# Holding two loads behind crossbar transposes, and another order for pairs 2 to 4, in a fused linear-attention and MLP kernel

## The chip, the cores and the metric

The kernel runs on one core of a Trainium2 chip. The metric is the device time of one execution in microseconds, as the median of several runs. Beside it there is the profile of one execution.

The engines are called TensorE (PE in the profile; its weight loads PEld), VectorE (DVE), ScalarE (ACT), GpSimd (POOL) and SyncE (SP). Each takes its instructions in order. A wait at the head of an engine's queue holds everything behind it.

## The reference

Two computations follow each other. The first is a gated linear attention over 4 batches, 8 heads, 768 tokens and head size 48:

```python
for t in range(S):
    state = alpha[:, :, t, :, None] * state + np.einsum('bhd,bhe->bhde', k[:, :, t], v[:, :, t])
    y[:, :, t] = np.einsum('bhd,bhde->bhe', q[:, :, t], state)
```

Its result, with the heads side by side, is x with 3072 rows of 384 numbers. The second is an MLP over these rows: `gelu(x @ w_in) @ w_out`, with an inner width of 2048 and the tanh form of GELU. Inputs and output are 32-bit floats in the chip's DRAM.

## The kernel before

**Tiles.** The 768 tokens are cut into 6 chunks of 128. A chunk of two batches is a pair: pair m is chunk m // 2 with batches 0 and 1 (m even) or 2 and 3 (m odd). There are 12 pairs, 0 to 11.

**Work of a pair.** The tiles a, q, k and v are loaded. `ln` takes the logarithm of a (tile la), `cum` sums it over the tokens with a matmul, and `b` and `binv` are the exponentials of the sum and of its negative. From these come q' = q * b (`qp`) and k' = k * binv (`kp`). q' and k' are transposed, on TensorE with a copy to SBUF for pairs 0 to 5 (`t`, `ev`, the tile qkT), and by a DMA transpose through the crossbar for pairs 6 to 11 (`turn6.0` is q' of pair 6, `turn6.1` its k', `turn6.2` its x). `attn` multiplies k' with q' (tile at) and q' with the state carried from the chunk before (tile yps), `mask` puts zeros above the diagonal (atm), `y` adds atm times v to yps, and `x` copies the result to SBUF, in two halves. `kv`, `tr` and `st` make the next state. x is transposed, on TensorE (`tx`, `xe`) or by the crossbar, into the tile xT.

**The MLP.** It runs per chunk in blocks of one batch (chunk 0) or two. `l1` is the first matrix product, in groups of six matmuls of 128x256 into the tile hT; `gelu` writes gT; `l2` is the second product in groups of four matmuls of 128x384 into the tile acc; `ot` copies acc to an output tile, and `store` writes that to DRAM. In a name like `l210.3` the digits after `l2` are the chunk, the first batch and the group; `ot03.0` is the output tile of chunk 0, batch 3.

**Buffers.** There are four PSUM buffers ff (for hT, acc and half of at), one ca of two banks (for cum and the other half of at), two yk; five SBUF buffers each for a, q, k, v and ot, and three xT.

**Order.** Nothing is scheduled by a tool. The list `FIRST` names each step with its engine (P, V, A, G, S for PE, DVE, ACT, POOL, SP), and each engine takes its steps in the order of the list. Semaphores between the engines follow from which tile each step reads and writes. ScalarE changes between a table with the logarithm and the exponential and one with GELU, at the steps where the list asks for it.

**Loads.** GpSimd issues all loads from pair 2 on, and a good part of the stores. It has eight semaphores for its transfers, used in turn, so that a transfer waits for the landing of the eighth before it. `LOADS` sets which tiles are loaded in which rows, and what they wait for: after `window 3` each load has a `gate` ahead of it, a copy of one element out of the tile that was loaded three loads earlier. GpSimd so waits until that tile has landed, and no more than three loads are under way.

Of the kernel before, what the change touches and what calls it, by code (L numbers as in the profile page):

```python
# [76 lines left out]
class _Kernel:  # L77
# [5 lines left out]
             "aqkv 3", "aqkv 4", "aqkv 5", "window 3", "aqkv 6", "aqkv 7", "aqkv 8", "aqkv 9", "aqkv 10", "aqkv 11")  # L83
# [24 lines left out]
        V:mask3.0 V:mask3.2 A:ln4.0 P:l211.1 P:l210.0 P:l211.2 P:y3.1 P:cum4.0 P:y3.0 P:l210.1 P:l211.3 V:x3.0 A:x3.1 A:b4.0 A:ln5.0 A:binv4.0
        A:ot11.0 P:tx3.0 P:tx3.1 P:l210.2 V:qp4.0 V:xe3.0 V:xe3.1 V:tr4.0 P:kv3.1 P:cum5.0 P:l210.3 P:l112.0 P:l112.1 V:st3.1 V:kp4.0 P:t4.0 V:tr4.2
        V:tr4.1 V:ev4.0 V:tr4.3 V:ev4.1 A:b5.0 A:ot10.0 A:binv5.0 P:l112.4 P:l112.7 A:gelu12.0 A:gelu12.1 P:kv4.0 P:l112.5 P:kv4.1 P:l112.3 A:gelu12.7  # L110
        A:gelu12.4 A:gelu12.3 A:gelu12.5 V:st4.0 V:st4.1 P:l112.6 A:gelu12.6 P:l112.2 P:attn4.0 G:gate.a6.0 G:load.v6.0 G:gate.q6.0 G:load.a7.0
        G:gate.k6.0 G:load.q7.0 G:store11.0 G:gate.v6.0 G:load.k7.0 G:gate.a7.0 G:load.v7.0 G:gate.q7.0 G:load.a8.0 G:gate.k7.0 V:kp5.0 V:tr5.0
        A:gelu12.2 P:l212.0 P:l212.1 V:mask4.2 V:mask4.0 V:mask4.1 P:l212.2 P:y4.0 P:l212.3 V:mask4.3 P:y4.1 A:ln6.0 P:cum6.0 A:x4.0 P:l213.0 V:tr5.1
        V:qp5.0 A:ot12.0 A:x4.1 P:tx4.0 V:xe4.0 A:binv6.0 P:tx4.1 V:xe4.1 P:l213.1 P:t5.0 V:kp6.0 V:ev5.0 A:b6.0 P:l213.2 P:l213.3 V:tr6.0 A:ev5.1
        P:attn5.0 V:tr6.1 G:store02.0 A:ln7.0 V:ot13.0 V:mask5.0 V:mask5.1 P:l120.0 V:mask5.2 V:tr6.2 V:mask5.3 P:l120.2 V:tr5.2 V:tr5.3 A:gelu20.0
        A:gelu20.2 P:l120.6 P:l120.7 A:gelu20.6 P:l120.1 A:gelu20.1 P:y5.0 V:x5.0 P:l120.4 A:gelu20.7 A:gelu20.4 P:l120.5 P:l120.3 A:gelu20.5 V:qp6.0
        V:tr6.3 G:load.q8.0 G:gate.v7.0 G:load.k8.0 S:turn6.1 A:gelu20.3 P:cum7.0 P:y5.1 V:x5.1 P:l221.0 P:kv5.0 P:l220.0 P:tx5.1 P:l221.1 V:st5.0
        G:gate.a8.0 G:load.v8.0 G:gate.q8.0 G:load.a9.0 V:xe5.1 A:b7.0 P:l220.1 P:tx5.0 P:kv6.0 V:qp7.0 V:xe5.0 S:turn6.0 P:l221.2 V:st6.0 P:kv5.1
        A:binv7.0 S:turn7.0 V:st5.1 A:ln8.0 P:cum8.0 A:binv8.0 A:b8.0 P:l221.3 P:l220.2 P:l220.3 A:ot21.0 P:attn6.0 V:kp7.0 A:ot20.0 P:l122.0 P:l122.2
        G:store21.0 V:mask6.0 V:mask6.1 V:mask6.2 V:mask6.3 P:l122.7 A:gelu22.0 A:gelu22.2 P:l122.4 V:tr7.0 V:tr7.1 G:store13.0 G:store12.0 P:y6.0  # L120
        A:gelu22.4 A:gelu22.7 P:l122.1 P:y6.1 A:gelu22.1 A:x6.0 P:l122.6 V:x6.1 P:l122.3 G:store10.0 P:kv6.1 V:st6.1 P:l122.5 P:l223.0 A:gelu22.3
        P:l223.1 A:gelu22.6 A:gelu22.5 P:l223.2 S:turn7.1 G:store20.0 S:turn6.2 G:gate.k8.0 V:qp8.0 G:load.q9.0 P:l222.0 V:tr7.2 V:tr7.3 V:kp8.0
        P:l222.1 S:turn8.0 P:attn7.0 V:mask7.2 V:mask7.3 P:l223.3 A:ln9.0 P:l222.2 P:l222.3 G:gate.v8.0 G:load.k9.0 G:gate.a9.0 G:load.v9.0
        G:gate.q9.0 G:load.a10.0 G:gate.k9.0 G:load.q10.0 G:gate.v9.0 V:mask7.0 V:mask7.1 A:ot23.0 A:ot22.0 P:cum9.0 P:l130.0 P:y7.0 P:l130.2 P:y7.1
        P:l130.4 V:x7.0 A:binv9.0 V:x7.1 V:tr8.0 V:tr8.1 A:gelu30.0 A:gelu30.2 P:l130.1 A:gelu30.4 A:gelu30.1 P:l130.3 V:kp9.0 A:gelu30.3 P:l130.5
        P:kv7.0 A:gelu30.5 P:l130.7 S:turn8.1 A:gelu30.7 G:load.k10.0 G:gate.a10.0 G:load.v10.0 G:gate.q10.0 G:load.a11.0 P:l130.6 P:kv7.1 P:l231.0
        V:st7.1 P:l231.1 P:l230.0 P:l230.1 A:gelu30.6 A:b9.0 V:tr8.2 V:tr8.3 V:st7.0 P:l231.2 P:l231.3 A:ot31.0 P:l230.2 P:l230.3 A:ot30.0 V:tr9.0
        V:qp9.0 G:gate.k10.0 S:turn7.2 P:attn8.0 P:l132.0 P:l132.5 V:mask8.0 V:mask8.1 P:l132.7 P:l132.2 V:mask8.2 V:mask8.3 V:tr9.1 A:gelu32.0 P:y8.0
        A:gelu32.5 A:gelu32.7 S:turn9.1 S:turn9.0 G:store30.1 P:l132.1 P:y8.1 P:l132.3 P:l132.6 V:x8.0 A:gelu32.2 P:l132.4 P:kv9.0 A:x8.1 V:tr9.2
        V:tr9.3 V:st9.0 A:gelu32.1 A:gelu32.3 A:gelu32.4 P:l232.0 P:l232.1 A:gelu32.6 P:l232.2 P:kv8.1 P:kv8.0 P:l233.0 P:l233.1 S:turn8.2 G:store23.0  # L130
        A:ln10.0 P:cum10.0 A:b10.0 G:store31.1 S:store30.0 V:st8.1 V:st8.0 S:store22.0 S:store31.0 A:binv10.0 V:qp10.0 P:l232.3 A:ot32.0 P:l233.2
        P:l233.3 V:ot33.0 P:attn9.0 A:ln11.0 P:l140.0 V:mask9.0 V:mask9.1 V:mask9.2 P:l140.7 P:l140.4 A:gelu40.0 A:gelu40.4 A:gelu40.7 V:kp10.0
        V:mask9.3 P:l140.1 P:l140.2 P:y9.0 P:l140.3 S:store32.1 S:turn10.0 A:gelu40.1 A:gelu40.3 S:turn10.1 V:x9.0 A:gelu40.2 P:y9.1 P:l240.0 A:x9.1
        P:l140.5 A:gelu40.5 P:l240.1 P:l140.6 P:kv9.1 V:st9.1 A:gelu40.6 P:l240.2 P:cum11.0 P:l240.3 S:turn9.2 G:load.q11.0 G:gate.v10.0 G:load.k11.0
        G:gate.a11.0 V:ot40.0 A:b11.0 P:l241.0 P:l241.1 P:l241.2 P:l241.3 G:store40.0 A:binv11.0 V:qp11.0 V:ot41.0 P:l142.0 P:attn10.0 V:mask10.0
        V:mask10.1 P:l142.5 A:gelu42.0 A:gelu42.5 P:l142.3 P:l142.6 A:gelu42.3 P:l142.2 A:gelu42.2 A:gelu42.6 P:l142.1 V:kp11.0 A:gelu42.1 S:turn11.0
        S:store41.0 S:turn11.1 P:l142.7 V:mask10.2 P:y10.0 V:mask10.3 P:y10.1 P:l142.4 P:l242.0 A:x10.0 A:x10.1 S:turn10.2 P:l243.0 P:l242.1
        A:gelu42.4 A:gelu42.7 P:l243.1 P:l242.2 P:l242.3 P:l243.2 P:l243.3 G:load.v11.0 A:ot42.0 S:store33.1 S:store32.0 P:attn11.0 V:ot43.0
        V:mask11.0 V:mask11.1 P:l150.0 P:l150.1 P:l150.6 A:gelu50.0 A:gelu50.1 A:gelu50.6 P:l150.4 P:l150.3 A:gelu50.3 V:mask11.2 V:mask11.3 P:y11.0
# [110 lines left out]
    def wait(self, r, m, j):  # L250

        u = self.p[list(self.p)[m]]
        return lambda e: self.nc.gpsimd.tensor_copy(self.gate[:, 0:1], u["T"][:, j, 0, 0, 0:1] if r == "T" else u["vb" if r == "v" else r][:, j, 0, 0:1])
# [385 lines left out]
    def tasks(self):  # L639
# [8 lines left out]
        loads, held = self.loads()  # L648
# [222 lines left out]
```

## Time and profile before

| | us |
|---|---|
| median of 3 runs | 173.23 |
| lowest, highest | 173.20, 173.99 |
| the profiled execution | 173.67 |
| its span, first to last instruction | 171.9 |
| TensorE busy in the span | 166.4 |
| VectorE busy | 108.7 |
| ScalarE busy | 126.4 |
| GpSimd busy | 74.0 |

How to read the profile: an entry of a timeline gives the start from the span's begin, the length, the engine, the line of the kernel, and what is written from what. Neighbours of the same kind are merged (x12), and the idle time of the engine ahead of an entry stands in square brackets with what ended it. Matmuls are pipelined, so that the length of one entry overlaps the start of the next by some 0.17 us. What TensorE loses shows in the distance from one start to the next. For a DMA, the entry is its issue, and its landing is told by the view of a tile. POOLq and SPq are the parts of an engine that only issue and wait.

### The profile page before, as it was taken

What the parts mean: (1) busy time and instruction counts of PE and PEld (TensorE: products, weight loads), DVE (VectorE), ACT (ScalarE), POOL (GpSimd) and SP (SyncE); (2) the same over time, 40 slices, a digit from 0 to 9 for tenths busy, and PEclk for the clock granted to TensorE, in tenths of its full rate; (3) what the DMA queues carried; (4) which work ended last, traced back from release to release, by engine and by line L of the source; (5) the groups of instructions that cost most, each with busy time, mean ns of one, the idle gap of its engine ahead of it and who ended that gap; (6) DMA issues with size and microseconds to landing.
All of it is one profiled execution on the core that took longest, in us unless ns stands there. A gap on an engine that the chain in (4) does not pass through costs nothing.

```text
span 171.9 us, 4766 instructions
## 1 busy us (share of the span) xinstructions
PE 166.4 (97%) x1998; PEld 131.5 (76%) x1998; DVE 108.7 (63%) x207; ACT 126.4 (74%) x203; POOL 74.0 (43%) x105
## 2 busy tenths in 40 slices
PE   7999999999999999999999899999999999999992
PEld 2678998567976886797696597796796895987971
DVE  6599602699997999999978666766944730620000
ACT  4696879896797989889788398587978682454740
POOL 6598458976238786841193614227000400100000
PEclk9999999999999999999999999999999999999998
DMA  4999999999999899999499999999962793130103
GB/s 134 286 231 174 228 251 259 233 212 194 262 235 185 209 176 233 205 205 149 92 264 222 129 148 217 78 141 285 254 105 50 91 191 95 46 91 5 46 24 115
DMA packets 54213, 29.01 MB, mean 169 GB/s; under 512 B 43728, under 2 KB 50176, under 8 KB 54192
## 3 DMA queue, kind: packets, MB, share of 16 engines
q0 software_dynamic: 31296, 19.96, 73.4%
q1 hardware_dynamic: 22352, 8.36, 25.4%
q10 hardware_dynamic: 544, 0.39, 0.8%
q8 instruction: 15, 0.25, 0.6%
q14 instruction: 6, 0.05, 0.1%
HBM read 25.17 MB, written 4.72 MB: 174 GB/s over the span
## 4 chain that ended last, share of the span: by engine, by line
PE 81%; DVE 7%; DMA 5%; ACT 4%; issue 1%; DVEq 0%; ACTq 0%
PE hT L557 34%; PE acc L576 28%; DMA xT<-x 5%; PE at L446 3%; PE idle L228 3%; PE cum L285 2%; PE yps L525 2%; PE kv L475 2%; PE xT_ps L515 1%; DVE atm L465 1%; PE cum L317 1%; DVE tr L489 1%; PE qkT_ps L364 1%; DVE kp L354 1%; DVE stmp L500 1%
## 5 line engine op out<-in xcount | busy, mean ns | idle before, releaser
L557 PE MATMUL hT<-xT,w_in 128*128 128x256 bf16 (+1 forms) x672 | 69.8, 258 | 0.5 <-DMA xT<-x 0.5
L576 PE MATMUL acc<-w_out,gT 128*128 128x384 bf16 (+3 forms) x416 | 68.2, 314 | 0.0
L563 ACT ACTIVATE gT<-hT 128x512 bf16<-128x512 f32 x96 | 52.9, 599 | 16.1 <-PE hT L557 14.9
L557 PEld LDWEIGHTS <-w_in 128*128 128x128 bf16 x672 | 61.8, 113 | 1.9 <-DMA xT<-x 0.9
L576 PEld LDWEIGHTS <-gT 128*128 128x128 bf16 x416 | 37.4, 98 | 20.5
L465 DVE TENSOR_TENSOR atm<-at,ut 128x512 bf16<-128x512 f32 x48 | 30.3, 684 | 2.8 <-PE at L446 2.7
L601 POOL DMA_DIRECT2D out_dram<-ot x15 | 8.4, 562 | 32.9 <-DVE ot L588 25.6
L588 DVE COPY ot<-acc 128x384 f32<-128x384 f32 (+1 forms) x10 | 5.2, 523 | 25.9 <-PE acc L576 25.6
L588 ACT COPY ot<-acc 128x384 f32<-128x384 f32 (+2 forms) x16 | 7.3, 458 | 13.0 <-PE acc L576 9.5
L500 DVE TENSOR_TENSOR stmp<-kv,st 128x384 f32<-128x384 f32 x16 | 8.9, 557 | 9.1 <-PE kv L475 8.6
L489 DVE STREAM_TRANSPOSE tr<-b 32x256 f32<-32x256 f32 x32 | 14.0, 438 | 0.8
L247 POOL DMA_DIRECT2D a<-in_alpha_dram x11 | 12.2, 1112 | 4.6 <-issue 1.7
L354 DVE TENSOR_TENSOR kp<-k,binv 128x768 bf16<-128x768 f32 (+1 forms) x15 | 11.9, 794 | 2.6 <-DMA k<-in_k_dram 1.9
L247 POOL DMA_DIRECT2D k<-in_k_dram x11 | 12.3, 1118 | 2.9 <-issue 1.3
L219 ACT ACT_TABLE_LOAD x10 | 12.8, 1283 | 0.9 <-PEq L855 0.7
L247 POOL DMA_DIRECT2D vb<-in_v_dram x11 | 12.2, 1107 | 2.5 <-DMA q<-in_q_dram 1.0
L247 POOL DMA_DIRECT2D q<-in_q_dram x11 | 12.3, 1115 | 1.7 <-DMA w_in<-in_moe_w_in_dram 1.0
L563 ACT ACT_TABLE_LOAD x10 | 12.8, 1283 | 0.2
L354 DVE TENSOR_TENSOR qp<-q,b 128x768 bf16<-128x768 f32 (+1 forms) x15 | 11.9, 795 | 0.9 <-ACT b L343 0.6
L343 ACT ACTIVATE b<-cum 128x768 f32<-128x768 f32 (+1 forms) x15 | 10.1, 684 | 2.6 <-PE cum L317 2.2
L343 ACT ACTIVATE binv<-cum 128x768 bf16<-128x768 f32 (+1 forms) x15 | 10.3, 688 | 2.2 <-PE cum L317 1.3
L535 DVE CAST x<-yps 128x384 bf16<-128x384 f32 x12 | 6.5, 555 | 6.1 <-PE yps L525 6.0
(75 smaller groups left out, 156.8 us busy)
## 6 DMA issues: line engine op xcount, KB each, us to landing
a<-in_alpha_dram POOLq DMA_DIRECT2D x9, 384.0 KB, 9.4
q<-in_q_dram POOLq DMA_DIRECT2D x9, 384.0 KB, 7.3
k<-in_k_dram POOLq DMA_DIRECT2D x9, 384.0 KB, 8.0
out_dram<-ot POOLq DMA_DIRECT2D x12, 192.0 KB, 4.0
vb<-in_v_dram POOLq DMA_DIRECT2D x9, 192.0 KB, 6.8
w_in<-in_moe_w_in_dram POOLq DMA_DIRECT2D x4, 384.0 KB, 8.6
w_out<-in_moe_w_out_dram POOLq DMA_DIRECT2D x4, 384.0 KB, 9.9
out_dram<-ot SPq DMA_DIRECT2D x7, 192.0 KB, 2.1
```

What stands on the lines that cost most here:

```text
L219: nc.scalar.add_instruction(mybir.InstLoadActFuncSet(name=nc.get_next_instruction_name(), act_func_set_id=i, engine=mybir.EngineType.Activ ...
L247: dma(u[t][:, lo:hi].rearrange("t b h d -> t (b h) d"), src.rearrange("b h s d -> s (b h) d")[c * C:(c + 1) * C])
L343: self.nc.scalar.activation(u[n].rearrange("t i h d -> t i (h d)")[:, lo:hi], cum, AF.Exp, scale=1.0 if n == "b" else -1.0)
L354: self.nc.vector.tensor_tensor(out, rows, b, op=ALU.mult)
L465: self.nc.vector.tensor_tensor(u["atm", i][:, o], u["at", i][o], self.ut[:, None, :].to_broadcast([self.C, self.H // 2, self.C]), op=ALU.mult)
L489: self.nc.vector.transpose(u["tr"][f:f + 32, :, 0:32], rows[:, lo:lo + H * 2 * D].rearrange("t (g n) -> t g n", n=2 * D)[:, :, 0:32])
L500: nc.vector.tensor_tensor(s, acc, old, op=ALU.add)
L557: self.nc.tensor.matmul(h[:, s].rearrange("p (g t) -> p g t", t=self.C), w_in[:, j, nt % 4 + s], self.xT[c % self.NX][:, lo:hi, j], start= ...
L563: return lambda e: self.nc.scalar.activation(self.gT[c % self.NG][:, nt:nt + 4 // (hi - lo), lo * self.C:hi * self.C], f.pop(("h", c, lo, ...
L576: self.nc.tensor.matmul(f["acc", c, b][:, lo:hi], self.gT[c % self.NG][:, nt, b * self.C:(b + 1) * self.C], self.w_out[:, nt, lo:hi], star ...
L588: self.copy(e)(f["ot", c, b][:, sl], f["acc", c, b] if half is None else f["acc", c, b, half][:, sl])
L601: return lambda e: (self.nc.sync if e == "SP" else self.nc.gpsimd).dma_start(self.out[r:r + self.C, sl], f["ot", c, b][:, sl])
```

## The change

Three things change. First, the steps of the list between the transposes of pair 2 and the MLP's second block of chunk 1 stand in another order: on TensorE, VectorE and ScalarE groups change places, and five copies that VectorE made are made by ScalarE (the output tiles `ot01`, `ot02`, `ot03`, the second half of x of pair 2, the first half of x of pair 3). The stores of the output tiles 00, 03 and 11 are issued by SyncE and not by GpSimd. Second, GpSimd loads a, q, k and v pair by pair from pair 3 on, and `window 3` begins with pair 8 and not with pair 6, so that the tiles of pairs 6 and 7 are loaded without a gate. Third, two new gates stand in GpSimd's queue: `gate.T6.0` reads the transposed q' of pair 6 ahead of the load of a of pair 9, and `gate.X6.0` reads the transposed x of pair 6 ahead of the loads of k and v of pair 9. All later steps stay as they are.

```diff
@@ LOADS
-             "aqkv 3", "aqkv 4", "aqkv 5", "window 3", "aqkv 6", "aqkv 7", "aqkv 8", "aqkv 9", "aqkv 10", "aqkv 11")
+             "aqkv 3", "aqkv 4", "aqkv 5", "aqkv 6", "aqkv 7", "window 3", "aqkv 8", "gate T 6 0", "aq 9", "gate X 6 0", "kv 9", "aqkv 10", "aqkv 11")
@@ FIRST
...
-        G:store03.0 G:gate.v5.0 G:load.k6.0 S:store01.0 V:qp3.0 P:tx2.0 P:tx2.1 P:l202.3 V:xe2.0 V:xe2.1 P:kv2.0 P:l110.0 P:l110.7 P:l110.1 V:kp3.0
...
+        V:xe2.1 V:xe2.0 P:kv2.0 P:l110.0 P:l110.6 V:kp3.0 V:st2.0 V:tr3.0 V:tr3.1 P:l110.5 A:ot02.0 A:gelu10.0 A:gelu10.6 P:t3.0 S:store00.0 P:l110.3
...
@@ def wait(self, r, m, j):
-        return lambda e: self.nc.gpsimd.tensor_copy(self.gate[:, 0:1], u["T"][:, j, 0, 0, 0:1] if r == "T" else u["vb" if r == "v" else r][:, j, 0, 0:1])
+        c, i = list(self.p)[m]
+        src = {"T": lambda: u["T"][:, j, 0, 0, 0:1], "X": lambda: self.xT[c % self.NX][:, 2 * i, 0, 0:1]}.get(r, lambda: u["vb" if r == "v" else r][:, j, 0, 0:1])
+        return lambda e: self.nc.gpsimd.tensor_copy(self.gate[:, 0:1], src())
@@ def tasks(self):
                 xts[c, 2 * i] = xts[c, 2 * i + 1] = xe
+                if ("X", m, 0) in held:
+                    held["X", m, 0].deps.append(xe)
```

On VectorE, from the state rows of pair 2 (`tr`) to the first state of pair 2 (`st`), the order before was this; b_100 belongs to pair 3, kp_98 is its k', and xT_104 is the xT tile of chunk 1:

```order
L489 STREAM_TRANSPOSE tr<-b_99 32x8x32 x4
L588 COPY ot<-acc 128x384 x2
L465 TENSOR_TENSOR atm<-at,ut 128x512 x4
L588 COPY ot<-acc 128x384
L535 CAST x<-yps 128x8x48 x2
L354 TENSOR_TENSOR qp_94<-q,b_100 128x16x48
L548 COPY xT_104<-xT_ps 128x384 x2
L354 TENSOR_TENSOR kp_98<-k,binv 128x16x48
L500 TENSOR_TENSOR stmp<-kv,st_1_81 128x384
L502 TENSOR_TENSOR st_0_80<-stmp,tr 128x384
L588 COPY ot<-acc 128x384
```

And this is the same stretch in the changed kernel (its lines are numbered one higher):

```order
L490 STREAM_TRANSPOSE tr<-b_99 32x8x32 x4
L589 COPY ot<-acc 128x384
L466 TENSOR_TENSOR atm<-at,ut 128x512 x4
L536 CAST x<-yps 128x8x48
L355 TENSOR_TENSOR qp_94<-q,b_100 128x16x48
L549 COPY xT_104<-xT_ps 128x384 x2
L355 TENSOR_TENSOR kp_98<-k,binv 128x16x48
L501 TENSOR_TENSOR stmp<-kv,st_1_81 128x384
L503 TENSOR_TENSOR st_0_80<-stmp,tr 128x384
```

Three copies of output tiles and one half of x have left this stretch. On ScalarE the stretch from the transposes of pair 2 to the first GELU of chunk 1 was this before (la_88, b_100 and binv are of pair 3, gT_107 is of chunk 1):

```order
L385 COPY qkT<-qkT_ps 128x16x64 x2
L219 ACT_TABLE_LOAD
L300 ACTIVATE la_88<-a 128x16x48
L343 ACTIVATE b_100<-cum 128x768
L343 ACTIVATE binv<-cum 128x768
L563 ACT_TABLE_LOAD
```

In the changed kernel it reads:

```order
L386 COPY qkT<-qkT_ps 128x16x64 x2
L589 COPY ot<-acc 128x384
L218 ACT_TABLE_LOAD
L301 ACTIVATE la_88<-a 128x16x48
L344 ACTIVATE b_100<-cum 128x768
L536 CAST x<-yps 128x8x48
L344 ACTIVATE binv<-cum 128x768
L589 COPY ot<-acc 128x384 x2
L564 ACT_TABLE_LOAD
```

The four copies stand here, one ahead of the logarithm and three ahead of the first GELU. On GpSimd, from the load of v of pair 8 to that of v of pair 9, the order before was this; ot x5 are five stores:

```order
L247 DMA vb<-in_v_dram 128x16x48
L253 COPY gate<-q 128x1
L247 DMA a<-in_alpha_dram 128x16x48
L601 DMA out_dram<-ot 128x384 x5
L253 COPY gate<-k 128x1
L247 DMA q<-in_q_dram 128x16x48
L253 CAST gate<-vb 128x1
L247 DMA k<-in_k_dram 128x16x48
L253 COPY gate<-a 128x1
L247 DMA vb<-in_v_dram 128x16x48
```

And in the changed kernel:

```order
L246 DMA vb<-in_v_dram 128x16x48
L254 CAST gate<-qkT 128x1
L254 COPY gate<-q 128x1
L246 DMA a<-in_alpha_dram 128x16x48
L602 DMA out_dram<-ot 128x384 x5
L254 COPY gate<-k 128x1
L246 DMA q<-in_q_dram 128x16x48
L254 CAST gate<-xT_103 128x1
L254 CAST gate<-vb 128x1
L246 DMA k<-in_k_dram 128x16x48
L254 COPY gate<-a 128x1
L246 DMA vb<-in_v_dram 128x16x48
```

The two gates on qkT and xT_103 are new; everything behind them in GpSimd's queue, the five stores and the loads of pair 10 too, waits until they pass.

More of the change, by code (lines that the diff above doesn't have):

```diff
@@ L108 @@
[L108 to L139, printed above, removed]
@@ new lines @@
+        P:tx3.0 V:xe3.0 V:tr4.1 P:cum5.0 G:load.a7.0 G:load.q7.0 G:load.k7.0 G:load.v7.0 G:gate.q7.0 G:load.a8.0 G:gate.k7.0 A:b5.0 S:store03.0
+        P:l210.3 P:l112.0 P:l112.7 S:store11.0 A:ot10.0 A:binv5.0 V:kp4.0 A:gelu12.0 A:gelu12.7 V:tr4.2 V:tr4.3 P:t4.0 V:ev4.0 P:l112.3 P:l112.5
+        V:ev4.1 P:kv4.0 P:l112.4 A:gelu12.3 P:kv4.1 A:gelu12.5 A:gelu12.4 V:st4.0 P:l112.6 A:gelu12.6 S:store01.0 P:l112.1 P:l112.2 A:gelu12.1 V:st4.1
+        V:tr5.0 V:kp5.0 P:attn4.0 A:gelu12.2 P:l212.0 P:l212.1 V:mask4.2 V:mask4.0 V:mask4.1 P:l212.2 P:y4.0 P:l212.3 V:mask4.3 P:y4.1 A:ln6.0
@@ new lines @@
+        P:cum6.0 A:x4.0 P:l213.0 V:tr5.1 V:qp5.0 A:ot12.0 A:x4.1 P:tx4.0 V:xe4.0 A:binv6.0 P:tx4.1 V:xe4.1 P:l213.1 P:t5.0 V:kp6.0 V:ev5.0 A:b6.0
+        P:l213.2 P:l213.3 V:tr6.0 A:ev5.1 P:attn5.0 V:tr6.1 G:store02.0 A:ln7.0 V:ot13.0 V:mask5.0 V:mask5.1 P:l120.0 V:mask5.2 V:tr6.2 V:mask5.3
+        P:l120.2 V:tr5.2 V:tr5.3 A:gelu20.0 A:gelu20.2 P:l120.6 P:l120.7 A:gelu20.6 P:l120.1 A:gelu20.1 P:y5.0 V:x5.0 P:l120.4 A:gelu20.7 A:gelu20.4
+        P:l120.5 P:l120.3 A:gelu20.5 V:qp6.0 V:tr6.3 G:load.q8.0 G:gate.v7.0 G:load.k8.0 S:turn6.1 A:gelu20.3 P:cum7.0 P:y5.1 V:x5.1 P:l221.0 P:kv5.0
@@ new lines @@
+        P:l220.0 P:tx5.1 P:l221.1 V:st5.0 G:gate.a8.0 G:load.v8.0 V:xe5.1 A:b7.0 P:l220.1 P:tx5.0 P:kv6.0 V:qp7.0 V:xe5.0 S:turn6.0 G:gate.T6.0
+        G:gate.q8.0 G:load.a9.0 P:l221.2 V:st6.0 P:kv5.1 A:binv7.0 S:turn7.0 V:st5.1 A:ln8.0 P:cum8.0 A:binv8.0 A:b8.0 P:l221.3 P:l220.2 P:l220.3
+        A:ot21.0 P:attn6.0 V:kp7.0 A:ot20.0 P:l122.0 P:l122.2 G:store21.0 V:mask6.0 V:mask6.1 V:mask6.2 V:mask6.3 P:l122.7 A:gelu22.0 A:gelu22.2
+        P:l122.4 V:tr7.0 V:tr7.1 G:store13.0 G:store12.0 P:y6.0 A:gelu22.4 A:gelu22.7 P:l122.1 P:y6.1 A:gelu22.1 A:x6.0 P:l122.6 V:x6.1 P:l122.3
@@ new lines @@
+        G:store10.0 P:kv6.1 V:st6.1 P:l122.5 P:l223.0 A:gelu22.3 P:l223.1 A:gelu22.6 A:gelu22.5 P:l223.2 S:turn7.1 G:store20.0 S:turn6.2 G:gate.k8.0
+        V:qp8.0 G:load.q9.0 G:gate.X6.0 P:l222.0 V:tr7.2 V:tr7.3 V:kp8.0 P:l222.1 S:turn8.0 P:attn7.0 V:mask7.2 V:mask7.3 P:l223.3 A:ln9.0 P:l222.2
+        P:l222.3 G:gate.v8.0 G:load.k9.0 G:gate.a9.0 G:load.v9.0 G:gate.q9.0 G:load.a10.0 G:gate.k9.0 G:load.q10.0 G:gate.v9.0 V:mask7.0 V:mask7.1
+        A:ot23.0 A:ot22.0 P:cum9.0 P:l130.0 P:y7.0 P:l130.2 P:y7.1 P:l130.4 V:x7.0 A:binv9.0 V:x7.1 V:tr8.0 V:tr8.1 A:gelu30.0 A:gelu30.2 P:l130.1
@@ L145 @@
+        P:l152.0 P:l152.5 A:gelu52.0 A:gelu52.5 P:l152.2 A:gelu52.2 P:l152.1 A:gelu52.1 P:l152.3 A:gelu52.3 P:l152.7 P:l152.4 P:l152.6 A:gelu52.4
+        P:l252.0 P:l252.1 P:l252.2 A:gelu52.7 A:gelu52.6 P:l252.3 S:store50.0 A:ot52.0 S:store52.0 S:store51.0 P:l253.0 P:l253.1 A:ot53.0 S:store53.0
+        P:l253.2 P:l253.3 P:l253.4 A:ot53.1 S:store53.1 P:l253.5 V:ot53.2 G:store43.0 S:store53.2
     """.split()
```

34 lines of the change are left out of this document (23 added, 11 removed).

## The prediction

> **What bounds the kernel now.** I read the page first, for the engine that is full.
>
> ```profile
> core 0: 171.9 us, clock 0.996
> ```
> ```profile
> PE 166.4 (97%) x1998; PEld 131.5 (76%) x1998; DVE 108.7 (63%) x207; ACT 126.4 (74%) x203; POOL 74.0 (43%) x105
> ```
>
> TensorE is busy for 166.4 of 171.9 us at a clock of 0.996, and the change removes none of its instructions. So it can gain only the moments in which TensorE stands still or stretches, and it can lose by adding such moments. The list of TensorE's waits has one inside the program that is not its start:
>
> ```profile
> PE hT L557 <- DMA xT<-x: 0.5, 1, 0.5
> ```
>
> The chain of waits from 84 to 120 us says where this is. Its third column is the length of a piece; I also take the unit prices of eight yps matmuls (0.20) and of six hT matmuls (0.67) from it.
>
> ```profile
> 88.28 0.20 PE yps L525 x8
> 88.48 0.67 PE hT L557 x6
> ...
> 90.29 8.05 DMA xT<-x
> ```
>
> From 90.29 on the chain is one transfer: the crossbar transpose of pair 6's x, 8.05 us from its issue to its landing. TensorE's own timeline shows what it cost:
>
> ```profile
> 97.39 0.49 PE L317 MATMUL cum<-la,ut_h 128*128 128x384 f16 x2
> 98.38 0.85 PE L557 MATMUL hT<-xT,w_in 128*128 128x256 bf16 x6 [0.51 <-DMA xT<-x]
> ```
>
> The second place is no wait by name. In the chain from 48 to 70 us the path leaves TensorE and runs through VectorE, piece after piece, from the first row below to the second, before it comes back:
>
> ```profile
> 54.19 0.96 DVE qp L354
> ...
> 64.81 2.50 DVE atm L465 x4
> ...
> 67.62 0.33 PE cum L317 x2
> 67.95 0.65 PE acc L576 x4
> ```
>
> The stretch from 36 to 68 us, in which pairs 2 to 4 are worked on, has this row (length, then busy time of PE, PEld, DVE, ACT, POOL, each with its count, then clock, DMA share and GB/s):
>
> ```profile
> 36.00:68.00 32.00, 31.79 (x427) 24.43 (x425) 29.71 (x54) 26.95 (x39) 20.75 (x27) 1.00 1.28 215
> ```
>
> VectorE is busy for 29.71 of 32 us, ScalarE for 26.95. VectorE has hardly a gap left, and TensorE's rows show small stretches where it hands over late:
>
> ```profile
> 60.22 0.82 PE L557 MATMUL hT<-xT,w_in 128*128 128x256 bf16 x6
> 61.09 0.33 PE L475 MATMUL kv<-vb,kp 128*128 128x96 bf16 x4
> ...
> 64.07 2.12 PE L576 MATMUL acc<-w_out,gT 128*128 128x384 bf16 x12
> 66.15 0.37 PE L525 MATMUL yps<-vb,atm 128*128 128x48 bf16 x8
> 66.36 0.81 PE L576 MATMUL acc<-w_out,gT 128*128 128x384 bf16 x4
> 67.01 0.61 PE L525 MATMUL yps<-vb,atm 128*128 128x48 bf16 x8
> 67.46 0.48 PE L317 MATMUL cum<-la,ut_h 128*128 128x384 f16 x2
> ```
>
> **The change, part by part.** *The gate on x of pair 6.* Two cum matmuls take 0.33 us, so the first hT group of chunk 3 could have begun at 97.39 + 0.33 = 97.72; it began at 98.38. That is 0.66 us lost. While the crossbar is under way, GpSimd's timeline has these loads:
>
> ```profile
> 89.24 1.17 POOL L247 DMA_DIRECT2D k<-in_k_dram  x1
> 90.41 0.20 POOL L253 COPY gate<-a 128x1 f32<-128x1 f32 x1
> 90.53 1.15 POOL L247 DMA_DIRECT2D vb<-in_v_dram  x1
> ```
>
> These are k and v of pair 9, which the change holds until x of pair 6 has landed. The next two rows are the time to landing of that x transpose and of the one for pair 9, at whose issue no load was under way:
>
> ```profile
> DMA to landing us min/median/max: 8.0/8.0/8.0
> ```
> ```profile
> DMA to landing us min/median/max: 2.7/2.7/2.7
> ```
>
> So with k and v out of its way the crossbar lands between 90.29 + 2.7 = 93.0 and, if the load of q of pair 9 just ahead is what slows it, 98.3. I take about 95, since two of the three loads beside it are gone, and a landing anywhere before 97.7 gains the whole 0.66 us. What is late next there? The group after needs masks and output copies that are already done, so nothing I can name; the 0.66 stands, with 0 as its other end.
>
> A rule of the Trainium skill speaks against this gate. In "DMA: Bandwidth & Descriptors", section "Rules for kernel authors", it says that transposes from different queues have to be serialized, but that "A transpose next to ordinary DMAs needs nothing". It speaks of data, not of speed; read as a rule on time, the 0.66 us would be nothing and the sum 172.8. The rows of 8.0 against 2.7 us speak against that reading.
>
> The price of the gate is that GpSimd stands behind it: k of pair 9 is issued at about 95.5 and not at 89.24, and v, then a and q of pair 10, follow it. Of what that may cost, below, in the rivals.
>
> *The gate on q' of pair 6.* GpSimd now waits for that transpose before it loads a of pair 9. Before, it did this:
>
> ```profile
> 77.02 1.16 POOL L247 DMA_DIRECT2D a<-in_alpha_dram  x1 [0.30 <-issue]
> 85.11 2.72 POOL L601 DMA_DIRECT2D out_dram<-ot  x5 [6.93 <-ACT ot L588]
> ```
> ```profile
> 78.03 4.91 SPq L422 DMA_TRANSPOSE qkT<-qp  x2
> ```
>
> After that load GpSimd idled 6.93 us, until the output tile of the first of five stores was written. q' of pair 6 is issued at 78.03, the first of the two in the last row, and with the two landing times above it lands between 80.7 and 86.0. The load of a therefore moves into the idle stretch, at worst 2 us past its end. Nobody on TensorE's path waits for it soon. I cost it at nothing; without that idle stretch it would push the stores and q of pair 9 back by its own 1.16 us, with no TensorE work behind them.
>
> *The order of pairs 2 to 4.* Five copies go from VectorE to ScalarE: three output tiles and two halves of x. The groups of that stretch give the two prices:
>
> ```profile
> L588 DVE COPY ot<-acc 128x384 f32<-128x384 f32 x4 | 2.2, 554 | 0.3 <-PE acc L576 0.2
> ```
> ```profile
> L588 ACT COPY ot<-acc 128x384 f32<-128x384 f32 x3 | 1.4, 479 | 0.2 <-PE acc L576 0.2
> ```
>
> x copies have the same shape, so I take the same prices. VectorE falls by 5 x 0.554 = 2.8 us to 26.9, ScalarE rises by 5 x 0.479 = 2.4 us to 29.3. The two change places: what was tight on VectorE gets loose, and ScalarE is next. TensorE's losses from the late VectorE are, with the unit prices above: kv at 61.09 could follow at 60.22 + 0.67 = 60.89, lost 0.20; yps at 66.15 could follow twelve acc matmuls (3 x 0.65 = 1.95) at 66.02, lost 0.13; cum at 67.46 could follow at 67.01 + 0.20 = 67.21, lost 0.25. Together 0.58 us. All of it gone is one end. The other is that all 2.4 us of ScalarE's new work come out on TensorE. I take 0.15 us of new loss, near the first end, for two reasons: ScalarE's moved copies lie mostly where it had gaps waiting for TensorE, and cum of pair 4, the step behind ScalarE's logarithm, stands an acc group and a yps group earlier than before, which is where the small loss will be. Net gain 0.43 us.
>
> *Loads of pairs 3 to 7 and the stores.* The loads now stand pair by pair, and those of 6 and 7 are no longer held. The transfers were not idle in this stretch (share 1.28 above), so the same bytes land at about the same rate, in an order that suits the use better; each remains ahead of its user. Three stores move from GpSimd's queue to SyncE's, where the store that was there already now stands behind them; SyncE is through with all four some 10 us before its first crossbar, and the output tiles they free are needed later still. I cost all this at nothing. What covers it is the distance between landing and use; if it were gone, a load would cost its delay at TensorE directly.
>
> *Sum.* 0.66 + 0.43 = 1.09 us less. The profiled execution took 173.67 us, 1.77 of them around the span; it would take 172.6. It lies 0.44 above the median of the runs, 173.23, from which the same sum gives 172.1 us.
>
> **The rivals.** *Only one gain arrives* (no change). Either q of pair 9 and the five stores suffice to keep the crossbar of x late, or ScalarE takes back the 0.43. For it: both engines are above 84% busy in 36 to 68, and one load still lies ahead of the crossbar. Against: the landing has 2.7 us to spare from my 95. The time is 173.23 - 0.43 = 172.8 or 173.23 - 0.66 = 172.6.
>
> *The loads behind the gate come too late* (slower). The place is the attention of pair 9, in these rows: GpSimd's load of v of pair 10, its time to landing, SyncE's issue of q' of pair 9, that one's time to landing, and TensorE's first use.
>
> ```profile
> 105.58 1.16 POOL L247 DMA_DIRECT2D vb<-in_v_dram  x1 [0.34 <-issue]
> ```
> ```profile
> DMA to landing us min/median/max: 10.9/10.9/10.9
> ```
> ```profile
> 109.43 1.66 SPq L422 DMA_TRANSPOSE qkT<-qp  x1
> ```
> ```profile
> DMA to landing us min/median/max: 9.2/9.2/9.2
> ```
> ```profile
> 122.28 0.62 PE L446 MATMUL at<-qkT 64*128 64x128 bf16 x16
> ```
>
> v lands at 105.58 + 10.9 = 116.5 and q' behind it at 109.43 + 9.2 = 118.6; with the gains TensorE wants it at 122.28 - 1.09 = 121.2. So it decides from 2.6 us of delay on. The gate moves k of pair 9 by some 6 us. If 5 us of this reached q' of pair 9, TensorE would wait 123.6 - 121.2 = 2.4 us, and the time is 173.23 - 1.09 + 2.4 = 174.5. For it: loads and crossbars beside each other crawl here. Against: the transfers that come earlier leave the queues emptier, so a later issue need not be a later landing.
>
> *ScalarE becomes the bound* (slower). If 1.8 of its 2.4 new us came out on TensorE, in place of the 0.15 I take: 173.23 - 0.66 - 0.58 + 1.8 = 173.8.
>
> **How the numbers follow.** The limit of 0.5%, about what a measurement of this kernel can tell from no change, is 0.87 us: faster begins below 172.36, slower above 174.10; the last rival's 173.8 is its middle, and it reaches over that limit in part. My forecast has 0.58. Its own range goes from 171.6 (all of 0.58 and 0.66, which is 172.0, and 0.4 for small losses of the same kind that I have not counted) to 172.6, and of it 0.45 lies under 172.36 and 0.13 above. One gain only: 0.20, all within. The late loads: 0.13, slower. ScalarE's bound: 0.09, of which 0.04 is within and 0.05 slower. That makes faster 0.45, same 0.37, slower 0.18. The range, with the forecast's lower end, goes from 171.6 to 174.1, which leaves out the late loads and the far part of ScalarE's bound.
>
> **What would show it.** Right: x of pair 6 lands before 97, TensorE has no wait on xT<-x, and the chain does not pass through that transfer; from 36 to 68 VectorE falls to about 27 us and ScalarE rises to about 29; cum of pair 6 follows its yps group without a gap. Wrong: a TensorE wait for a crossbar at a later pair, q' of pair 9 above all; or a chain that runs through ScalarE between 40 and 60 us; or a load of pairs 3 to 7 that lands after its use begins to wait.

## The result, and the profile after

The changed kernel takes 172.27 us (median of 20 runs, 171.50 to 173.52). The kernel before takes 173.87 us in 20 runs beside it (172.80 to 176.66). The ratio is 0.9908, with a 95% interval of 0.9885 to 0.9931: 1.2 to 2.0 us less. The forecast was 1.09 us less.

The page of the profiled execution of the changed kernel, its spans and busy times:

```profile
core 0: 171.0 us, clock 1.000
```
```profile
PE 165.6 (97%) x1998; PEld 130.9 (77%) x1998; DVE 106.6 (62%) x202; ACT 128.0 (75%) x208; POOL 71.5 (42%) x96
```

VectorE has given 2.1 us away and ScalarE has taken 1.6. The span alone misleads, though, because the two executions did not reach the changed part at the same time. These are TensorE's timelines of before and of after where the transposes of pair 2 begin; up to there TensorE's steps are the same:

```profile
33.86 0.55 PE L378 MATMUL qkT_ps<-ident,qp 64*128 64x64 bf16 x16
```
```profile
34.80 0.55 PE L379 MATMUL qkT_ps<-ident,qp 64*128 64x64 bf16 x16
```

And these are VectorE's timelines of both at the other end, the last copy of an output tile:

```profile
168.59 0.23 DVE L588 COPY ot<-acc 128x64 f32<-128x64 f32 x1 [16.88 <-PE acc L576]
```
```profile
168.36 0.23 DVE L589 COPY ot<-acc 128x64 f32<-128x64 f32 x1 [16.88 <-PE acc L577]
```

After starts 0.94 us later, and over all kernels here this start varies from 33.6 to 36.5 us. From there to the last copy it takes 133.56 us where before took 134.73, which is 1.17 us less. From the copy to the end of the span it takes 2.6 us where before took 3.3. This last gain was not forecast.

What the prediction named can be read row by row. First the crossbar transpose of pair 6's x in the changed kernel, its issue on SyncE's queue and its time to landing:

```profile
L429 SPq DMA_TRANSPOSE xT<-x x1: 1211/1211/1211, 90.8 to 90.8; - x1
DMA to landing us min/median/max: 4.5/4.5/4.5
```

TensorE's timeline at the place where that x is used:

```profile
97.86 0.49 PE L318 MATMUL cum<-la,ut_h 128*128 128x384 f16 x2
98.18 0.82 PE L558 MATMUL hT<-xT,w_in 128*128 128x256 bf16 x6
```

x landed at 95.2, the hT group follows cum after 0.32 us where it followed after 0.99, and no wait stands behind it. Next the windows of after from 36 to 68 us (length, busy time of PE, PEld, DVE, ACT and POOL, clock, DMA share, GB/s):

```profile
36.00:68.00 32.00, 31.88 (x430) 24.59 (x428) 27.90 (x50) 29.22 (x44) 16.42 (x15) 1.00 1.35 220
```

VectorE has fallen from 29.71 to 27.90 us and ScalarE has risen from 26.95 to 29.22. TensorE's timeline of after at the three places that the prediction summed, and at the one it expected to get worse:

```profile
51.82 1.14 PE L577 MATMUL acc<-w_out,gT 128*128 128x384 bf16 x6
52.99 0.48 PE L318 MATMUL cum<-la,ut_h 128*128 128x384 f16 x2
...
59.77 1.50 PE L558 MATMUL hT<-xT,w_in 128*128 128x256 bf16 x12
61.11 0.33 PE L476 MATMUL kv<-vb,kp 128*128 128x96 bf16 x4
...
64.92 2.12 PE L577 MATMUL acc<-w_out,gT 128*128 128x384 bf16 x12
66.88 0.36 PE L526 MATMUL yps<-vb,atm 128*128 128x48 bf16 x8
67.08 0.81 PE L577 MATMUL acc<-w_out,gT 128*128 128x384 bf16 x4
67.73 0.36 PE L526 MATMUL yps<-vb,atm 128*128 128x48 bf16 x8
67.94 0.48 PE L318 MATMUL cum<-la,ut_h 128*128 128x384 f16 x2
```

kv, yps and cum of pair 6 (67.94) follow without a gap. cum of pair 4 (52.99) stands 1.17 us behind the start of six acc matmuls that take 6 x 0.16 = 0.97 us, so 0.20 is lost there. Before, that step lost something too, which the prediction did not list. TensorE's timeline of before:

```profile
52.42 0.36 PE L525 MATMUL yps<-vb,atm 128*128 128x48 bf16 x8
52.77 0.49 PE L317 MATMUL cum<-la,ut_h 128*128 128x384 f16 x2
```

That is 0.35 - 0.20 = 0.15 us. GpSimd's timeline of after shows both gates:

```profile
82.76 0.18 POOL L254 CAST gate<-qkT 128x1 f32<-128x1 bf16 x1 [6.79 <-DMA qkT<-qp]
...
83.44 1.16 POOL L246 DMA_DIRECT2D a<-in_alpha_dram  x1
85.59 2.71 POOL L602 DMA_DIRECT2D out_dram<-ot  x5 [0.98 <-ACT ot L589]
...
95.37 0.18 POOL L254 CAST gate<-xT 128x1 f32<-128x1 bf16 x1 [5.78 <-DMA xT<-x]
...
96.00 1.17 POOL L246 DMA_DIRECT2D k<-in_k_dram  x1 [0.20 <-issue]
```

The first gate takes up idle time ahead of the five stores, which still begin at 85.6. The second holds k of pair 9 until 96.0.

### The profile page after: what moved, and what is told of

It is laid out like the page before. It is cut to its first block, busy times and chain, and to the rows that moved or that the text cites. A ratio compares the mean times of both kernels' runs of the same rounds, so it can differ in the third digit from the quotient of the medians.

```text
span 171.0 us, 4765 instructions
## 1 busy us (share of the span) xinstructions
PE 165.6 (97%) x1998; PEld 130.9 (77%) x1998; DVE 106.6 (62%) x202; ACT 128.0 (75%) x208; POOL 71.5 (42%) x96
## 4 chain that ended last, share of the span: by engine, by line
PE 85%; DMA 8%; ACT 3%; SPq 2%; POOL 1%; issue 0%; DVE 0%; POOLq 0%
PE hT L558 37%; PE acc L577 34%; DMA wide<-in_v_dram 5%; PE at L447 3%; DMA k<-in_k_dram 3%; PE yps L526 2%; PE cum L318 2%; PE kv L476 2%; SPq L243 2%; PE yps L456 1%; ACT qkT L386 1%; PE qkT_ps L379 1%; PE xT_ps L545 1%; PE xT_ps L516 1%; ACT L564 1%; ACT binv L344 1%
## 5 line engine op out<-in xcount | busy, mean ns | idle before, releaser
L589 DVE COPY ot<-acc 128x384 f32<-128x384 f32 (+1 forms) x7 | 3.6, 510 | 25.8 <-PE acc L577 25.8
L602 POOL DMA_DIRECT2D out_dram<-ot x12 | 6.6, 556 | 29.1 <-DVE ot L589 27.8
L589 ACT COPY ot<-acc 128x384 f32<-128x384 f32 (+2 forms) x19 | 8.8, 461 | 13.2 <-PE acc L577 9.7
L503 DVE TENSOR_TENSOR st<-stmp,tr 128x384 bf16<-128x384 f32 x16 | 8.9, 558 | 0.6
```

The costliest lines, as they stand in the source:

```text
L503: nc.vector.tensor_tensor(new, acc, end[:, :, None].to_broadcast([C, H // 2, 2 * D]), op=ALU.mult)
L589: self.copy(e)(f["ot", c, b][:, sl], f["acc", c, b] if half is None else f["acc", c, b, half][:, sl])
```

## The experiments

Three distances carry most of what follows, all read from the trace of one execution. The stretch runs from the transposes of pair 2 to the start of the last group series of the MLP's second product (called the last projection). The end runs from there to the end of the span. The flight is the time from the issue to the landing of the crossbar transpose of pair 6's x. The ratio is that of the times to the kernel before in the same series.

| kernel | stretch | end | flight of x of 6 | ratio, 95% interval |
|---|---|---|---|---|
| before | 131.85 | 6.19 | 8.05 | 1 |
| before, second trace | 131.31 | 6.18 | 7.51 | |
| x_only | 131.52 | 6.19 | 4.94 | 0.9983, 0.9958 to 1.0008 |
| store1 | 131.43 | 5.68 | 7.60 | 0.9962, 0.9929 to 0.9995 |
| store3 | 131.67 | 5.56 | 7.86 | 0.9956, 0.9924 to 0.9988 |
| copies_on_V | 132.29 | 5.56 | 4.92 | 1.0008, 0.9971 to 1.0045 |
| order_only | 130.80 | 5.54 | 7.46 | 0.9923, 0.9896 to 0.9950 |
| stores_G | 130.68 | 6.19 | 4.51 | 0.9936, 0.9912 to 0.9960 |
| after | 130.68 | 5.55 | 4.48 | 0.9908, 0.9885 to 0.9931 |
| no_T | 130.68 | 5.55 | 4.02 | 0.9911, 0.9884 to 0.9938 |
| held67 | 130.69 | 5.55 | 4.45 | 0.9891, 0.9868 to 0.9914 |
| hold_v | 130.68 | 5.55 | 7.33 | 0.9882, 0.9858 to 0.9907 |
| hold_k | 130.69 | 5.54 | 7.06 | 0.9907, 0.9879 to 0.9935 |
| cum_late | 130.94 | 5.54 | 4.96 | 0.9886, 0.9854 to 0.9918 |

The end returns within 0.02 us between kernels that place the three stores alike. The stretch does so too, once the time is taken off that TensorE loses ahead of the first hT group of chunk 3: before, its second trace, store1 and store3 then all have 131.2. The flight varies from execution to execution, even of the same kernel. Medians of kernels in different series differ by more than that, so parts are told apart by the distances, and the ratios say whether the sum of them is real.

### x_only: the gate on x of pair 6 in the kernel before

```diff
-  "aqkv 9",
+  "aq 9", "gate X 6 0", "kv 9",
-  G:load.q9.0
+  G:load.q9.0 G:gate.X6.0
```

> The kernel before with the gate on x of pair 6 alone (ahead of k and v of pair 9). Theory of two separate gains: the gate is worth the 0.66 us wait, ratio to before about 0.996; x of pair 6 lands some 5 us after its issue and not 8, TensorE has no wait on xT<-x, and the losses between 60 and 68 us stay (0.58 us). Rival (the gate works only because the changed loads and the gate on q' leave the queues emptier): x still takes 7 to 8 us, ratio 1.000.

The flight fell from 8.05 to 4.94 us, against the rival, and the gap ahead of the hT group, 0.67 us in the trace of before, closed. But 0.31 us came back later, which the theory did not have. TensorE's timeline of this kernel at the first hT group of chunk 4, and the time to landing of the transpose of pair 8's x that it waits for:

```profile
121.83 0.62 PE L448 MATMUL at<-qkT 64*128 64x128 bf16 x16
122.29 0.36 PE L457 MATMUL yps<-st,qkT 64*128 64x48 bf16 x16
122.96 2.81 PE L559 MATMUL hT<-xT,w_in 128*128 128x256 bf16 x24 [0.31 <-DMA xT<-x]
```
```profile
DMA to landing us min/median/max: 8.4/8.4/8.4
```

In before the same transpose took 4.75 us and landed 3.4 us ahead of its use. GpSimd's loads of pair 11 now meet it: k of pair 11 is issued 0.26 us ahead of it here, at 114.21, where before issued it 3.0 us behind. In all nine kernels with the gate k of pair 11 is issued at most 0.3 us ahead of this transpose or at most 1.4 us behind it, and the flight is 6.15 to 8.44 us. In the five executions without the gate k is issued 1.4 us ahead or 3.0 us behind, and the flight is 4.75 to 5.45. So the gate that ends one collision of loads with the crossbar goes with another one, two pairs later.

The stretch is only 0.33 us shorter, and the ratio cannot be told from 1. The changed kernel runs close to the same wait: there x of pair 8 landed at 122.66 and was used at 122.81.

### order_only: the changed kernel without both gates

```diff
-  "gate T 6 0", "aq 9", "gate X 6 0", "kv 9"
+  "aqkv 9"
-  G:gate.T6.0
...
-  G:gate.X6.0
```

> The changed kernel without its two gates: order of pairs 2 to 4, store queues, loads of pairs 6 and 7 unheld. Theory of two separate gains: about 0.45 us less between 36 and 72 us, the wait of about 0.5 us on x of pair 6 stays, ratio to before about 0.9975. Rival (all of the gain is the gates'): ratio 1.000 and the same losses between 36 and 72 us as before.

The stretch is 1.05 us shorter than before. Up to cum of pair 9, ahead of which neither gate acts on TensorE, 63.53 us have become 63.06: the new order is worth 0.47. No run tries the regrouped loads of pairs 3 to 5 without it; the traces of before and after list no wait of TensorE, VectorE or ScalarE for a load between 34 and 69 us. The rest of the 1.05 us is the crossbar, although nothing holds the loads: the wait of about 0.5 us that the theory kept is not there. TensorE's timeline at the critical hT group:

```profile
97.11 0.49 PE L318 MATMUL cum<-la,ut_h 128*128 128x384 f16 x2
97.53 0.85 PE L558 MATMUL hT<-xT,w_in 128*128 128x256 bf16 x6
```

In this execution the flight was 7.46 us, and TensorE lost 0.42 - 0.33 = 0.09. So the gate could have gained about 0.1 us here, where the prediction had 0.66.

### before_again: a second trace of the kernel before

> The kernel before, once more, for a second trace. Asked is how far its landmarks vary from execution to execution: the start of the transposes of pair 2 (33.86 us in the first trace, 34.80 in the changed kernel's, with the same code up to there), the flight of x of pair 6 (8.05 us), the TensorE gap ahead of the first projection of stage 3 (0.66 us) and the end (6.19 us). Theory: the first varies by some 1 us, the other three stay within 0.3 us, 0.1 us and 0.1 us. Rival: the crossbar's 8 us are an accident of the first trace, x lands within 6 us and the gap is under 0.2; then the wait was worth nothing in the median.

The theory fell for the flight, which is 0.54 us shorter and not within 0.3, and for the gap. The rival was right on the gap alone: x did not land within 6 us. TensorE's timeline of this second execution, and its time to landing of x of pair 6:

```profile
97.16 0.49 PE L317 MATMUL cum<-la,ut_h 128*128 128x384 f16 x2
97.61 0.85 PE L557 MATMUL hT<-xT,w_in 128*128 128x256 bf16 x6
```
```profile
DMA to landing us min/median/max: 7.5/7.5/7.5
```

The crossbar is slow again, but it lost 0.45 - 0.33 = 0.12 us and not 0.66. Two more kernels below (store1, store3) have the order and loads of before at this place and lost 0.22 and 0.48, with flights of 7.60 and 7.86. These are TensorE's timelines of store1 and of store3:

```profile
98.12 0.49 PE L317 MATMUL cum<-la,ut_h 128*128 128x384 f16 x2
98.67 0.85 PE L557 MATMUL hT<-xT,w_in 128*128 128x256 bf16 x6
```
```profile
97.44 0.49 PE L317 MATMUL cum<-la,ut_h 128*128 128x384 f16 x2
98.25 0.85 PE L557 MATMUL hT<-xT,w_in 128*128 128x256 bf16 x6 [0.32 <-DMA xT<-x]
```

Over the four, the loss is the flight less 7.4 us: what is issued some 7.1 us ahead of cum and needed 0.33 behind it has 7.4 us for nothing. The gap in the trace of before was the largest of four.

### no_T: the changed kernel without the gate on q' of pair 6

```diff
-  "gate T 6 0", "aq 9",
+  "aq 9",
-  G:gate.T6.0
```

> The changed kernel without the gate on q' of pair 6; the gate on x stays. Theory of two separate gains: the load of a of pair 9 goes back to about 77 us, TensorE is no later anywhere, ratio to before 0.991 as with the change. Rival (the gate on q' carries part of the gain): a of pair 9 runs beside the crossbar of q' of pair 6, which lands later, TensorE waits for it or for k' behind it, ratio 0.994 or more.

Stretch and end are those of the changed kernel to 0.01 us. The gate on q' is worth nothing.

### copies_on_V: the five copies back on VectorE, in the new order

```diff
-  A:ot03.0 ... A:x2.1 ... A:ot01.0 ... A:ot02.0 ... A:x3.0
+  V:ot03.0 ... V:x2.1 ... V:ot01.0 ... V:ot02.0 ... V:x3.0
```

> The changed kernel with the five moved copies (three output tiles, two halves of x) back on VectorE at the same places of the order. Theory (the gain of the order is VectorE's relief): VectorE is busy about 29.7 of 32 us between 36 and 68 again, TensorE loses 0.4 to 1 us there, ratio to before 0.9935 to 0.997. Rival (the gain is the order of TensorE's groups or of the loads): no new loss, ratio 0.991.

The stretch is 1.61 us longer than the changed kernel's, more than the 0.4 to 1 us of the theory. It is 0.44 longer than before's in the table and 0.98 longer than that of its second trace. TensorE's timeline shows two waits for VectorE's copy of x, at places where the changed kernel loses nothing:

```profile
42.59 0.51 PE L545 MATMUL xT_ps<-ident,x 128*128 128x128 bf16 x6 [0.66 <-DVE x L536]
```
```profile
55.93 0.33 PE L476 MATMUL kv<-vb,kp 128*128 128x96 bf16 x4 [0.71 <-DVE x L536]
```

So the new order needs the copies of x on ScalarE; these two waits are 1.37 us of the 1.61. What the copies would be worth in the old order was not tried.

### stores_G: the three stores back on GpSimd

```diff
-  S:store00.0 ... S:store03.0 ... S:store11.0
+  G:store00.0 ... G:store03.0 ... G:store11.0
```

> The changed kernel with the three early stores (heads' rows 00, 03, 11) back on GpSimd's queue instead of SyncE's; order, loads and both waits as changed. Two things are asked. First the stretch from the transposes of pair 2 to the last output projection: theory (store queues are silent, costed at nothing): 1.15 us shorter than before, as in the changed kernel; rival (three stores of 96 KB each delay the loads on GpSimd's queue that stand behind them): less than 0.9. Second the end: from the start of the last projection to the end of the span it took 6.19 us before and 5.52 changed, and 5.55 to 5.60 in all kernels with the changed order and store queues. If the store queues give that 0.6 us (the end waits for every queue that was used late, or for code of an engine whose stream got longer), this kernel goes back to about 6.2 and its median to about 172.8; if the unheld loads or something else gives it, it stays at 5.55 and the median at 172.3.

The stretch stays at 130.68 (the three stores are 192 KB each by the profile, twice what the expectation says, and are silent there even so), and the end goes back from 5.55 to 6.19 us. The last gain belongs to the store queues.

### held67: pairs 6 and 7 held as before

```diff
-  "aqkv 6", "aqkv 7", "window 3", "aqkv 8",
+  "window 3", "aqkv 6", "aqkv 7", "aqkv 8",
...
+  G:gate.q5.0
   G:load.a6.0
...
```

> The changed kernel with the loads of pairs 6 and 7 held by window 3 as before (eight gates more on GpSimd); order, store queues and both waits as changed. Theory (the unheld loads are worth nothing in the stretch, costed at nothing): from the transposes of pair 2 to the last projection 1.1 to 1.2 us shorter than before, as in the changed kernel. Rival (GpSimd's gates delay the train of loads, k and v of pairs 6, 7 come later and collide with the crossbar): 0.3 to 0.6 us of it is lost. The end, 5.52 us from the start of the last projection to the end of the span in the changed kernel and 6.19 before: if GpSimd's shorter stream gives the 0.6 us, it is 6.2 here and the median about 172.8; if the store queues give it, 5.55 and 172.3.

Its profiled execution began 1.7 us late and at a clock of 0.99, so only the distances are read: 130.69 and 5.55. Loading pairs 6 and 7 unheld is worth nothing.

### store3 and store1: three stores, or one, on SyncE in the kernel before

```diff
-  G:store00.0 ... G:store03.0 ... G:store11.0
+  S:store00.0 ... S:store03.0 ... S:store11.0
```

> The kernel before with the three early stores (rows 00, 03, 11) on SyncE's queue instead of GpSimd's, and nothing else. Theory: the 0.6 us at the end are this alone, and come from SyncE's own stream. At the end SyncE waits for eight store semaphores one after another, 0.07 us each; in the traces so far one of its steps takes 0.46 us, always its 79th instruction, and each store on its queue puts two more instructions ahead and takes the next semaphore in turn. Three stores more put the 79th ahead of the last store's landing, where it costs nothing, and the last store on the last semaphore. So: from the start of the last projection to the end 5.55 us (6.19 before), TensorE's losses in the middle as before, median 0.65 us less than before. Rival (the end is shorter because GpSimd's queue carries less, or the gain needs the new order): 5.9 to 6.2, median within 0.2 of before.

In store1 only the first of the three is moved.

> The kernel before with one of the three stores alone (row 00) on SyncE's queue. Theory of SyncE's stream: two instructions more put its 79th on the wait ahead of the last store's, so 0.4 us of the refill is covered, and the last store moves by one of the semaphores, with two 0.07 us steps left behind it: 5.70 us from the start of the last projection to the end. Rival (the gain is in proportion to the stores moved): a third of 0.64, so 5.98. Rival (it needs all three): 6.19.

Both came out as SyncE's own stream says: an end of 5.56 us with three stores (5.55 expected) and of 5.68 with one (5.70 expected, 5.98 if the gain went with the number of stores). The trace shows how. At its end SyncE takes nine waits in a fixed order. In before they stand in this row of its line (times are the first and last start):

```profile
L866 SPq EVENT_SEMAPHORE  x9: 28/28/28, 169.3 to 171.0; - x9
```

The last store is issued at 168.84 and lands 1.5 us later, at 170.3. Of the nine, these start in the window from 170.3 to 170.45, and in that from 170.5 to 171.0:

```profile
L866 SPq EVENT_SEMAPHORE  x2: 28/28/28, 170.3 to 170.4; - x2
```
```profile
L866 SPq EVENT_SEMAPHORE  x2: 28/28/28, 170.9 to 171.0; - x2
```

The landing lets the sixth wait through, the seventh follows 0.07 us behind it, and then SyncE stands still for 0.46 us, although every store has landed. After, the nine are over at 170.1, when the last store lands:

```profile
L869 SPq EVENT_SEMAPHORE  x9: 28/28/28, 169.0 to 170.1; - x9
```
```profile
L869 SPq EVENT_SEMAPHORE  x2: 28/28/28, 169.0 to 169.5; - x2
```

The second row is the window from 168.9 to 169.6: the standstill now lies between the first two waits, while the last store is still under way. In each of the kernels whose end was followed instruction by instruction (before, after, x_only, stores_G, store1, store3) it stands ahead of the same place in SyncE's stream (place 79 of its recorded instructions, counted from 0). Each store moved to SyncE brings two instructions, so three move the waits by six places against it. They also take the next semaphores in turn, and the last store then belongs to the ninth wait, with none behind it. Of the 0.64 us, the standstill is about 0.4 and the three waits that no longer follow the landing are 3 x 0.07 = 0.2. What SyncE does in the 0.46 us, the trace does not name; the expectation's word refill is a guess that no run tests.

### hold_v and hold_k: one of the two loads held

```diff
-  "aq 9", "gate X 6 0", "kv 9"
+  "aqk 9", "gate X 6 0", "v 9"
```

> The changed kernel with k of pair 9 let out ahead of the second wait: only v of pair 9 waits for x of pair 6. What slows the crossbar is asked. If any load beside it does so, in proportion to what lies beside it: k alone is half of what was held, x of pair 6 takes 5.5 to 6.5 us from issue to landing (4.5 with both held, 7.5 to 8.0 with neither). If it is the load that is converted on the way (v, from float32 to bfloat16), x takes 4.5 to 5.0. If it is k, 7 to 8. In all three x lands at 95 to 98, and the time from the transposes of pair 2 to the last projection changes by at most 0.1 against the changed kernel: median 172.2 to 172.4.

In hold_k, v goes ahead of the gate and k stays behind it.

> The changed kernel with v of pair 9 let out ahead of the second wait: only k of pair 9 waits for x of pair 6. With k let out and v held x of pair 6 took 7.3 us from issue to landing, nearly what it takes with neither held (7.5 and 8.0), where both held give 4.5. If any one load that stands queued at the crossbar's issue costs so much, x takes 7 to 8 us here too; if it is k (its rows alone, loaded without conversion), 4.5 to 5. The time changes by at most 0.2 us against the changed kernel.

The times to landing of pair 6's x, in hold_v and in hold_k:

```profile
DMA to landing us min/median/max: 7.3/7.3/7.3
```
```profile
DMA to landing us min/median/max: 7.1/7.1/7.1
```

One load of either kind, issued about a microsecond ahead of the transpose, costs the crossbar nearly as much as two (7.5 to 8.05); with both held it takes 4.0 to 5.0, and q of pair 9 is issued 2.3 us ahead in all of them. Neither proportion nor the conversion of v explains it. How far ahead a load is issued seems to count: x of pair 8 took only 5.1 to 5.45 us in four executions in which k of pair 11 was issued 1.4 us ahead of it. No run varies that distance alone. Both still land just in time, so the stretch does not change: the second wait pays only where x would come later than that.

### cum_late: the step that still loses, moved

```diff
-  P:cum4.0 A:b4.0 V:mask3.0 V:mask3.1 V:qp4.0 P:l210.0
+  P:l210.0 P:cum4.0 A:b4.0 V:mask3.0 V:mask3.1 V:qp4.0
```

> The changed kernel with the first matmul group of the second layer's rows 10 (l210.0) moved ahead of the cumulative sums of pair 4, which wait 0.20 us there for ScalarE's logarithm. Theory: the 0.20 us go, TensorE has work while the logarithm is made, and what follows on ScalarE (the exponential of pair 4) starts 0.3 us later but has room: from the transposes of pair 2 to the last projection 0.15 to 0.2 us less than the changed kernel's 130.68. Rival: the exponential and the transposes of pair 4 become late in turn and the loss reappears there: 0 to 0.2 more. In the median either is inside the interval.

The rival was right, and by more than it said. The loss at cum went, and TensorE's timeline has a new one 1.8 us later, because kv waits for ScalarE's copy of x, which stands in ScalarE's order behind the exponential of the cum that now starts 0.46 us later:

```profile
54.07 0.36 PE L526 MATMUL yps<-vb,atm 128*128 128x48 bf16 x8
54.70 0.33 PE L476 MATMUL kv<-vb,kp 128*128 128x96 bf16 x4 [0.27 <-ACT x L536]
```

The stretch is 0.26 us longer than the changed kernel's.

## Why the prediction was right, and where it was not

**The sign and the time** were right: 172.1 us was forecast and 172.27 measured. Counted as a difference it was too small, 1.09 us against 1.2 to 2.0, since the kernel before took 173.87 us in 20 runs and not 173.23. That the time came so near is luck: the sum started 0.64 us too low (173.23 for 173.87), and its gain was 0.51 us too small (1.09 for 1.60). The traces give 0.47 (order) + 0.13 to 0.67 (crossbar) + 0.64 (end) = 1.24 to 1.78 us.

**The order of pairs 2 to 4.** Forecast 0.43 us, measured 0.47. The three gaps went as named. ScalarE's 29.22 us is what was forecast (29.3), and ScalarE did not become the bound. VectorE's 27.90 is 1.0 above the 26.9 forecast. All five copies have left it (202 instructions in place of 207, at 0.55 us each), and the lengths of its instructions add up to 2.8 us less over the whole span (115.4 before, 112.6 after). But they overlap in part, and the busy time, which counts an overlap once, fell by only 2.1. The new loss at cum of pair 4 is 0.20, not 0.15, but it takes the place of an old one of 0.15 that the sum had left out. A second new one is 0.08: the transposes of x of pair 2 begin at 42.55, and 41.82 + 0.65 = 42.47 was possible. With these the sum is 0.58 + 0.15 - 0.20 - 0.08 = 0.45; that 0.43 was so near is in part chance.

**The gate on x of pair 6.** The mechanism was right: the landing came at 95.2 (about 95 forecast), and TensorE's wait went. The size failed. "A landing anywhere before 97.7 gains the whole 0.66 us" took one execution's gap for the kernel's. Over four executions with that order the gap is 0.12, 0.22, 0.48 and 0.66 us, 0.37 in the mean; with the new order and no gates it was 0.09. Also "nothing I can name" was late next: x of pair 8 is, by 0.31 us in x_only, and in the changed kernel it lands only 0.15 us ahead of its use, where before it had 3.4 us. That is the price of the gate, and it came at another place than the rival on late loads looked.

The first rival's doubt, that q of pair 9 ahead of the transpose suffices to keep it late, fell in each kernel with both loads held (flights of 4.0 to 5.0 us). The late loads did not come at the attention of pair 9: v of pair 10 was issued at the same time and landed at 113.9, not 116.5.

The Trainium skill's sentence weighed there, in "DMA: Bandwidth & Descriptors", section "Rules for kernel authors" ("A transpose next to ordinary DMAs needs nothing"), is about data. Read as a rule on time, it does not agree with the flights here, 7.1 to 8.05 us beside k or v and 4.0 to 5.0 without; but by the same runs what that costs the kernel is 0 to 0.66 us.

**The gate on q', and the unheld loads,** were costed at nothing, and are worth nothing (no_T, held67).

**The stores** were costed at nothing too, and that step failed: "SyncE is through with all four some 10 us before its first crossbar" is true and beside the point. The three stores act 120 us later, on the last microseconds, where SyncE waits out its semaphores. That is 0.64 us, as much as any other part, and store1 and store3 show it apart from all else. The crossbar's share, 0.29 us too large against the mean gap, makes up for a part of the missing 0.64.

## What to carry to other kernels

A gap behind a DMA is flight less slack, and the flight varies: price it from several executions, and take the one trace's gap as one draw. When a load is held behind one transfer, look at which transfer the loads behind it then meet. Read the stretch behind the last result like any other, in order of the waits: which queue a store uses decides where it stands in them, even when the store itself is early. And where one engine is relieved, name the old losses at the moved steps as well as the new ones, or the sum counts only half of the exchange.

## What the runs showed of the hardware that was not expected

For x of pair 6, one load issued about 1 us ahead slows the crossbar nearly as much as two: 7.1 and 7.3 us with k or v of pair 9, 7.5 to 8.05 with both, 4.0 to 5.0 with neither (q of pair 9 is 2.3 us ahead in all), and 2.7 for x of pair 9 with no load under way. Loads somewhat further ahead cost less: 5.1 to 5.45 us for x of pair 8 with k of pair 11 issued 1.4 us before it. SyncE stands still for 0.46 us at the same place of its stream in each kernel followed, whatever it waits for there; and a wait that is already satisfied costs it 0.07 us.
